# A fused attention and feed-forward kernel: two more slots between the mask and the exponential from the seventh pair on

## The chip, the cores and the metric

The kernel runs on one NeuronCore of a Trainium2 chip. The metric is the device time of one execution in microseconds (us). Engine names are those of the profile: PE (TensorE, matrix products; PEld are its weight loads), ACT (ScalarE), DVE (VectorE), POOL (GpSimd), and SP, which here only issues DMAs. Each engine works through its own instructions in program order; semaphores order them against each other.

## The reference, cut to what matters

Attention with a threshold over 8 batches of 8 heads, 576 positions and 64 channels; its output goes through a feed-forward layer of 512 to 2048 to 512.

```
scores = scale * q @ k.T                          # 8 x 8 x 576 x 576
thresh = max(scores, -1) - tau
scores = where(scores >= thresh, scores, -1e9)
attn   = exp(scores - max(scores, -1)); attn /= sum(attn) + 1e-9
x      = heads side by side (attn @ v)            # 4608 x 512
h      = x @ w_in;  g = h - tanh(h);  out = g @ w_out
```

## The kernel before

**Tiles.** Heads are taken in pairs, 4 pairs to a batch, 32 pairs in all. A pair has 9 score tiles of 128 query rows by 576 keys (`TPP = 9`): eight regular ones and one in which both heads share the rows (64 each). So there are 288 tiles, numbered through. Two neighbouring tiles, an even one (kind A) and an odd one (kind B), make a *duo*: they share one mask result `z`, one turned tile `zT`, one `pT`.

**Steps of a tile.** `scores` (L387): PE forms the scores in high and low halves in PSUM (`psS`, from `kT` and the swapped copy `kS`), and DVE scales them into `sc` and takes the row maximum in the same instruction (L420). `shift` (L426): DVE makes the bias `nb`. `kink` (L439): ACT applies the threshold with a very steep Prelu and writes `z` (L447). Then `z` has to be turned so that keys lie on partitions. For the first six pairs (`on_pe`, L57) PE does that in `weights` (L466), and ACT's exponential reads PSUM (L475). From the seventh pair on (tiles 54 and up) `kink` of the odd tile issues one DMA transpose for the duo on the SP queue into a buffer of `zt_pool` (L454), and `weights` is one exponential for the duo on ACT (L483). `attend` (L488): PE multiplies by v into `psO` (L506, L513, L524). `norm` (L531) divides on DVE, `emit_x` (L551) turns the result on PE for the layer.

**The layer.** It works in blocks of 512 tokens, one per batch, and a last block of leftovers. An *h* step is four products into `psH` (L579), then tanh on ACT (`bend`, L592) and the subtraction on DVE (`shrink`, L598) into `g`. A *y* step is four products into `psY` (L605); every fourth is followed by a copy on DVE (L617) and a store issued on SP (L620). `PATTERN` writes by hand in which slot of a 36-slot block (four pairs) an h or a y stands; '-' is a slot with neither.

**The order of work** is one loop over slots (L852). Slot s does, in this order: scores of tile s + `AHEAD`; `kink` of tile s + `MASK`; `weights` of tile s + `SOONER` of its pair; the layer's step; the stores; `attend` of the tile whose weights were two slots (`LAG`) before; then whatever `plan` holds. A shared tile of kind A is put off one slot, so every 18 slots one slot has no scores and the next has two tiles of them. `plan` holds the preparation of q, k and v (loads, splitting on POOL in L228 to L232, turning, swapping `kT` into `kS` on POOL in L337), placed relative to `AHEAD`; so are the weights' loads. From the tenth pair on q and k are turned by DMA transposes on SP too (L315).

Counted from the slot of a tile's own scores, the steps before the change are:

| pairs | mask | exponential | attend |
|---|---|---|---|
| 1 to 4 | +3 | +4 | +6 |
| 5 and 6 | +3 | +8 | +10 |
| 7 to 32 | +3 | +8 | +10 |

The first layer block starts at slot 40 (when tile 48 is scored), each next block 36 slots later; after the last slot the remaining layer steps follow without attention.

Of the kernel before, what the change touches and what calls it, by code (L numbers as in the profile page):

```python
# [18 lines left out]
def kernel(  # L19
# [26 lines left out]
    HPAIR = H // 2  # L46
# [6 lines left out]
    NTILE = NPAIR * TPP  # L53
# [6 lines left out]

    W = 2 * S

    AHEAD = 8
    LDK = 16
    MASK = 5
    LAG = 2


# [30 lines left out]
    for i in range(6):  # L99
# [8 lines left out]
    pool = lambda name, bufs, **kw: ctx.enter_context(  # L108
        tc.tile_pool(name=name, bufs=bufs, **kw)
    )  # L110
# [3 lines left out]
    qk_pool = pool("qk", 3)  # L114
    sc_pool = pool("sc", AHEAD - MASK + 2)
    st_pool = pool("st", 12)
    z_pool = pool("z", 4)
    zt_pool = pool("zt", 6)
    p_pool = pool("p", 3)
    o_pool = pool("o", 2)  # L120
    wt_pool = pool("wt", 4)
# [218 lines left out]
    def turn_first(t, part):  # L340

        hl = hls[0, t[0]]
        c0, c1 = ((0, 5), (5, TPP))[part]
        pl, tag = (ps_y, "y") if t == "ks" else (ps_h, "h")
        ps = pl.tile([P, 5 * P], FP16, name=f"ps1_{t}", tag=tag)
        for c in range(c0, c1):
            o = ps[:, (c - c0) * P : (c - c0 + 1) * P]
            if t == "ks":
                for a in range(2):
                    turn_chunk(o[64 * a : 64 * a + 64, :], c, hl[:, c, 1 - a, :])  # L350
            else:
                turn_chunk(o, c, hl[:, c, :, :].rearrange("p a d -> p (a d)"))
        if part == 0:
            mats[0, t] = qk_tile(t)
        dst, n = mats[0, t][:, c0 * P : c1 * P], (c1 - c0) * P
        if part == 1 or t == "q":
            nc.scalar.copy(out=dst, in_=ps[:, 0:n])
        else:
            nc.vector.tensor_copy(out=dst, in_=ps[:, 0:n])
# [17 lines left out]
    def kind(i):  # L377

        return "AB"[i % 2]

    def place(i):

        p, j = divmod(i, TPP)
        j = j - p % 2
        return (p, None, 4) if j in (-1, 8) else (p, j // 4, j % 4)

    def scores(i):  # L387
        p, hh, t = place(i)
        qT, kT, kS = mats[p, "q"], mats[p, "k"], mats[p, "ks"]
        ps = ps_big.tile([P, 1024], F32, name="psS", tag="big")  # L390
        main, rem, lo = slice(0, 512), slice(512, 576), 0
        if kind(i) == "B":
            main, rem, lo = slice(512, 1024), slice(448, 512), 448
        if hh is None:
            qrem = REM
            if q_by_dma(p):
                qrem = (slice(512, 640, 2), slice(513, 640, 2))
            for n, kk in enumerate((kT, kS)):
                for dst, cols in ((main, main_keys), (rem, rem_keys)):
                    for hh in range(2):  # L400
                        nc.tensor.matmul(  # L401
                            out=ps[64 * hh : 64 * hh + 64, dst],
                            lhsT=qT[:, qrem[hh]], rhs=cols(p, kk, hh),
                            start=(n == 0), stop=(n == 1),
                        )
        else:
            lhs = qT[:, (5 * hh + t) * P : (5 * hh + t + 1) * P]
            for n, kk in enumerate((kT, kS)):
                for dst, cols in ((main, main_keys), (rem, rem_keys)):
                    nc.tensor.matmul(  # L410
                        out=ps[:, dst], lhsT=lhs, rhs=cols(p, kk, hh),
                        start=(n == 0), stop=(n == 1),
                    )
        sc = sc_pool.tile([P, S], F32, name="sc")
        if kind(i) == "B":
            mx = mxs[i] = mxs.pop(i - 1)
        else:
            mx = mxs[i] = mx3[i // 2 % len(mx3)]
        c = int(kind(i) == "B")
        nc.vector.tensor_scalar(  # L420
            out=sc, in0=ps[:, lo : lo + S], scalar1=SC, scalar2=None,
            op0=ALU.mult, op1=ALU.max, accum_out=mx[:, c : c + 1],
        )
        scs[i] = sc

    def shift(i):  # L426

        if kind(i) == "A":
            return
        mx = mxs.pop(i)  # L430
        nb = st_pool.tile([P, 9], F32, name="nb", tag="nb")
        nc.vector.tensor_scalar(  # L432
            out=nb.rearrange("p (a b) -> p a b", b=3)[:, :, 0:2],
            in0=mx.rearrange("p (a b) -> p a b", b=4)[:, :, 0:3],
            scalar1=-1.0, scalar2=tau, op0=ALU.mult, op1=ALU.add,
        )
        nbs[i - 1], nbs[i] = nb[:, 0:1], nb[:, 1:2]

    def kink(i):  # L439
        sc, nb = scs.pop(i), nbs.pop(i)  # L440
        if kind(i) == "B":
            zt = zs.pop(i - 1)
            z = zt[:, S:W]
        else:
            zt = zs[i] = z_pool.tile([P, W], BF16, name="z")
            z = zt[:, 0:S]
        nc.scalar.activation(  # L447
            out=z, in_=sc, func=ACT.Prelu, bias=nb, scale=1.0, alpha=STEEP
        )
        if on_pe(i):  # L450
            zts[i] = zt
        elif kind(i) == "B":
            zts[i] = zt_pool.tile([P, TPP, P], BF16, name="zT")
            nc.sync.dma_start_transpose(out=zts[i], in_=zt)  # L454
# [148 lines left out]
    def project(m, ms, part, ps, last, cols=slice(0, d_model)):  # L603
# [30 lines left out]
    LAST = 1  # L634

    PATTERN = lambda m: {
        0: '-h--h-hh--h-hh-h-hh-h--hh-h--hh-y-yy',
        B - 2: 'hyhyhyhyhyhyhyhyhyhyhyhyhyhyhyhy',
    }.get(m, 'h-yhyhhyhyyhyyhh-yhhyhhy-yhyyh-yyhhy')

# [88 lines left out]
    def w_cast():  # L729
        flat, wt, i, cols = loaded.pop(0)  # L730
        nc.gpsimd.tensor_copy(out=flat[:, i * cols : (i + 1) * cols], in_=wt)
# [52 lines left out]
    for p in range(DUAL, NPAIR):  # L784
        first = TPP * p - AHEAD
        at = lambda d, f: plan.setdefault(first - d, []).append(f)
# [11 lines left out]
    for p in range(1, DUAL):  # L798
        first = TPP * p - AHEAD
        for d, f in PREP[3 if p == 1 else 0 :]:  # L800
# [37 lines left out]
    for at in sorted(plan):  # L838
        if at < -AHEAD:
            plan.setdefault(-AHEAD, []).extend(plan.pop(at))  # L840

    SOONER = (4, 4, 4, 4, 0, 0, 0)
    kinks, wts, atts = {}, {}, {}
    for i in range(NTILE + 3):
        at = i - SOONER[min(i // TPP, 6)]
        atts.setdefault(at + LAG, []).append(i)
        if i < NTILE:
            wts.setdefault(at, []).append(i)  # L850
            kinks.setdefault(i // 2 * 2 + 2 - AHEAD if i < 4 else i - MASK, []).append(i)
    for s in range(-AHEAD, NTILE + LAG + 3):  # L852
        p, j = divmod(max(s, 0), TPP)
        if 0 <= s < NTILE and j == 2 + LAG and p % HPAIR == 0 and p >= HPAIR:
            assert not todo
            todo = [(s + i, step) for i, step in layers(stage, False, PATTERN(stage))]
            stage += 1
        if s == NTILE:
            todo = [(s + n, step) for n, step in enumerate(layers(stage, True))]
            stage += 1  # L860
        if 0 <= s + AHEAD - 1 < NTILE:
            shift(s + AHEAD - 1)

        n = s + AHEAD
        if 0 < n < NTILE and place(n)[1] is None and kind(n) == "B":
            scores(n - 1)
        if 0 <= n < NTILE and (place(n)[1] is not None or kind(n) == "B"):
            scores(n)
        if s == 1 - AHEAD:
            for t in ("k", "q", "ks"):  # L870
                turn_first(t, 1)
        for i in kinks.pop(s, []):
            kink(i)
        bend()
        for i in wts.pop(s, []):
            weights(i)
        while todo and todo[0][0] <= s < NTILE + FIRST:
            todo.pop(0)[1]()
        if s == 0:
            nc.vector.tensor_tensor(  # L880
                out=fold, in0=ident_bf[:, 0:64], in1=ident_bf[:, 64:P], op=ALU.add
            )
        shrink()
        for store in going:
            store()
        going = stores[:-1]
        del stores[:-1]
        for i in atts.pop(s, []):
            pp, jj = divmod(i, TPP)
            if i < NTILE:  # L890
                attend(i)
                odd = pp % 2
                if jj == 3 + odd:
                    norm(pp, 0)
                elif odd and jj in (0, 8):
                    norm(pp - (jj == 0), 1)
            if pp and jj == 1 + pp % 2:
                emit_x(pp - 1)
        for step in plan.pop(s, []):
            step()  # L900
        for _ in range(cast_when.count(s + AHEAD)):
            w_cast()
        for _ in range(load_when.count(s + AHEAD)):
            w_load(next(pieces))
# [56 lines left out]
```

## Time and profile before

| | us |
|---|---|
| three runs | 511.88, 507.43, 510.61 |
| median | 510.61 |
| the profiled execution | 504.09 |
| its span, first to last instruction | 502.3 |

| engine | busy us | share of the span | instructions |
|---|---|---|---|
| PE | 482.5 | 96% | 4292 |
| PEld | 270.5 | 54% | 4354 |
| ACT | 431.9 | 86% | 617 |
| DVE | 400.8 | 80% | 1151 |
| POOL | 292.2 | 58% | 390 |

The profile is of one execution. Matmuls overlap, so the mean length of one (379 ns for 512 columns) is longer than the distance from one to the next. The costliest groups of the page are the row maximum on DVE (L420, 288 times, mean 752 ns), the mask on ACT (L447, 288 times, 773 ns), the y products (L605, 373 ns), the duo's exponential (L483, 117 times, 1157 ns), the h products (L579, 379 ns) and the score products (L410).

### The profile page before, as it was taken

Reading aid. Unit: us, or ns where it says so; the run is one execution under the profiler, and the core shown is the slowest. Engines: PE = TensorE matmul, PEld = TensorE weight load, DVE = VectorE, ACT = ScalarE, POOL = GpSimd, SP = SyncE. Lnnn points to the kernel's source line nnn. Section 1 sums busy time; section 2 is a strip of 40 time slices with the busy share of each in tenths; the row PEclk is TensorE's granted clock in tenths of the full one; section 3 lists DMA queues with packets and bytes.
Section 4 is the critical chain, followed back from the end, with each engine's and each line's share of the span. In section 5 each row is a group of like instructions: output and inputs, shape, how many; then the busy total and the mean of one; then the engine's idle time right before and its main releaser. Section 6 shows DMA issues by size and latency. Waiting matters only on the chain.

```text
span 502.3 us, 12201 instructions
## 1 busy us (share of the span) xinstructions
PE 482.5 (96%) x4292; PEld 270.5 (54%) x4354; DVE 400.8 (80%) x1151; ACT 431.9 (86%) x617; POOL 292.2 (58%) x390
## 2 busy tenths in 40 slices
PE   8999899989999999999999999999999999999997
PEld 4667566555555555555555555555555555444444
DVE  5899978988889898988898889889888887544430
ACT  5999999899999999999999999999989999434330
POOL 8999999897765675576575765658556600000000
PEclk9999999999999999999999999999999999999999
DMA  6852558999999999999999999999999965311003
GB/s 208 261 162 91 189 167 229 209 202 229 223 207 243 247 246 222 223 251 212 239 218 249 247 213 215 258 217 249 235 196 228 226 119 116 88 42 43 36 29 84
DMA packets 232157, 95.02 MB, mean 189 GB/s; under 512 B 202784, under 2 KB 221472, under 8 KB 232096
## 3 DMA queue, kind: packets, MB, share of 16 engines
q1 hardware_dynamic: 211152, 72.58, 75.4%
q10 hardware_dynamic: 20944, 21.67, 15.7%
q8 instruction: 34, 0.56, 0.5%
q14 instruction: 27, 0.22, 0.1%
HBM read 36.70 MB, written 9.44 MB: 92 GB/s over the span
## 4 chain that ended last, share of the span: by engine, by line
PE 74%; POOL 9%; ACT 5%; issue 4%; DVE 4%; DMA 2%; SPq 1%; ACTq 0%; POOLq 0%
PE psY L605 23%; PE psH L579 19%; PE psS L410 18%; PE psO L513 5%; PE psHt L579 3%; DMA kraw<-in_k_dram 2%; PE psS L401 2%; POOL kS L337 2%; ACT z L447 2%; DVE sc L420 1%; PE psO L524 1%; ACT pT L483 1%; ACT pT L475 1%; DVE g L598 1%; PE psO L506 1%
## 5 line engine op out<-in xcount | busy, mean ns | idle before, releaser
L420 DVE TENSOR_SCALAR_CACHE_REDUCE sc<-psS 128x576 f32<-128x576 f32 x288 | 213.5, 752 | 25.5 <-PE psS L410 12.4
L447 ACT ACTIVATE z<-sc,nb 128x576 bf16<-128x576 f32 x288 | 217.3, 773 | 8.6 <-DVE nb L432 6.1
L605 PE MATMUL psY<-w_out_sb,g 128*128 128x512 bf16 (+1 forms) x564 | 140.8, 373 | 1.6 <-issue 0.2
L483 ACT ACTIVATE pT<-zT 128x1152 f16<-128x1152 bf16 x117 | 135.4, 1157 | 4.8 <-DMA zT<-z 3.3
L579 PE MATMUL psH<-xT,w_in_sb 128*128 128x512 bf16 x448 | 118.8, 379 | 4.2 <-issue 1.7
L337 POOL COPY kS<-kT 64x1152 f16<-64x1152 f16 x62 | 70.9, 1144 | 76.6 <-DMA kT<-khl 72.8
L598 DVE SCALAR_TENSOR_TENSOR g<-th,psH 128x512 bf16<-128x512 f32 x128 | 87.6, 684 | 27.3 <-ACT th L592 26.3
L410 PE MATMUL psS<-kT,qT 128*128 128x512 f16 (+1 forms) x512 | 104.4, 285 | 3.2 <-DVE sc L420 1.9
L410 PE MATMUL psS<-kS,qT 128*128 128x512 f16 (+1 forms) x512 | 104.6, 286 | 0.0
L410 PEld LDWEIGHTS <-qT 128*128 128x128 f16 x1024 | 72.5, 97 | 57.8 <-issue 4.1
L592 ACT ACTIVATE th<-psH 128x512 f32<-128x512 f32 x128 | 74.9, 585 | 20.9 <-PE psH L579 20.9
L605 PEld LDWEIGHTS <-g 128*128 128x128 bf16 x592 | 51.1, 98 | 54.6 <-DVE g L598 0.4
L579 PEld LDWEIGHTS <-w_in_sb 128*128 128x128 bf16 x576 | 49.0, 98 | 55.9 <-issue 4.6
L513 PE MATMUL psO<-vb,pT 128*128 128x65 bf16 x1024 | 53.3, 194 | 0.0
L513 PEld LDWEIGHTS <-pT 128*128 128x128 f16 x1024 | 44.2, 98 | 10.0
L232 POOL TENSOR_TENSOR qhl<-qraw,qhl 128x576 f16<-128x576 f32 x31 | 39.7, 1282 | 2.6
L232 POOL TENSOR_TENSOR khl<-kraw,khl 128x576 f16<-128x576 f32 x31 | 39.7, 1281 | 2.6
L475 ACT ACTIVATE pT<-psZ 128x512 f16<-128x512 bf16 (+1 forms) x54 | 35.1, 653 | 2.5 <-PE psZ L466 2.2
L617 DVE COPY yo<-psY 128x512 f32<-128x512 f32 (+1 forms) x31 | 21.1, 679 | 13.0 <-PE psY L605 12.4
L539 DVE TENSOR_TENSOR osb<-psO,rc 128x256 bf16<-128x256 f32 x64 | 27.2, 425 | 2.2
L506 PE MATMUL psO<-vb,pT 128*128 128x130 bf16 x128 | 28.1, 220 | 0.1
L228 POOL TENSOR_SCALAR qraw<-qraw 128x576 f32<-128x576 f32 x31 | 20.9, 673 | 12.5 <-DMA qraw<-in_q_dram 12.5
(77 smaller groups left out, 453.0 us busy)
## 6 DMA issues: line engine op xcount, KB each, us to landing
out_dram<-yo SPq DMA_DIRECT2D x32, 256.0 KB, 3.6
kraw<-in_k_dram ACTq DMA_DIRECT2D x24, 288.0 KB, 4.5
qraw<-in_q_dram ACTq DMA_DIRECT2D x24, 256.0 KB, 4.3
wt<-in_moe_w_in_dram SPq DMA_DIRECT2D x8, 512.0 KB, 4.3
wt<-in_moe_w_out_dram SPq DMA_DIRECT2D x8, 512.0 KB, 4.3
vraw<-in_v_dram ACTq DMA_DIRECT2D x24, 160.0 KB, 4.1
vraw<-in_v_dram ACTq DMA_DIRECT2D x24, 128.0 KB, 3.9
vraw<-in_v_dram SPq DMA_DIRECT2D x8, 256.0 KB, 3.5
```

The costliest lines, as they stand in the source:

```text
L232: nc.gpsimd.tensor_tensor(out=hl[:, :, 1, :], in0=x, in1=hl[:, :, 0, :], op=ALU.subtract)
L337: nc.gpsimd.tensor_copy(out=o, in_=i)
L410: nc.tensor.matmul(out=ps[:, dst], lhsT=lhs, rhs=cols(p, kk, hh), start=(n == 0), stop=(n == 1),)
L420: nc.vector.tensor_scalar(out=sc, in0=ps[:, lo : lo + S], scalar1=SC, scalar2=None, op0=ALU.mult, op1=ALU.max, accum_out=mx[:, c : c + 1],)
L447: nc.scalar.activation(out=z, in_=sc, func=ACT.Prelu, bias=nb, scale=1.0, alpha=STEEP)
L475: nc.scalar.activation(out=pt[:, off * P : (off + n) * P], in_=ps[:, 0 : n * P], func=ACT.Exp)
L483: nc.scalar.activation(out=pt[:, 0 : n * P], in_=zts.pop(i)[:, 0:n, :], func=ACT.Exp)
L513: nc.tensor.matmul(out=po[:, t - 1 + ab, :], lhsT=pt[:, blk * P : (blk + 1) * P], rhs=vb[:, hh, c, :], start=False, stop=(n == 7), skip_gr ...
L579: nc.tensor.matmul(out=ps, lhsT=w_in_sb[:, c, n * P : (n + 1) * P], rhs=xs[m][:, c, :] if m < B else xR[:, c, :, :], start=(c == 0), stop= ...
L592: nc.scalar.activation(out=th, in_=ps, func=ACT.Tanh)
L598: nc.vector.scalar_tensor_tensor(out=gs[m][:, n, :], in0=th, scalar=-1.0, in1=ps, op0=ALU.mult, op1=ALU.add,)
L605: nc.tensor.matmul(out=ps, lhsT=gs[m][:, n, ms * P : (ms + 1) * P], rhs=w_out_sb[:, n, cols], start=(n == 0), stop=(n == DF_C - 1),)
```

## The change

Scores go ten slots ahead instead of eight, and the mask seven instead of five. `SOONER` grows by two for the first six pairs, so that these keep their distances: in the table above their rows stay as they are. From the seventh pair on `SOONER` is 0 as before, so there the exponential comes 10 slots after the scores and the attend step 12. `zt_pool` has eight buffers instead of six; `sc_pool` keeps its five (`AHEAD - MASK + 2`). The first layer block starts at slot 38, which is again when tile 48 is scored, and its pattern is two slots longer, with its last three y steps later by one, two and two slots; the other blocks still start at slots 76, 112 and so on, now two slots later against the scores. The loop has two slots more. No instruction is added or removed; POOL's instructions keep their order.

```
-    AHEAD = 8
+    AHEAD = 10
-    MASK = 5
+    MASK = 7
...
-    zt_pool = pool("zt", 6)
+    zt_pool = pool("zt", 8)
...
     PATTERN = lambda m: {
-        0: '-h--h-hh--h-hh-h-hh-h--hh-h--hh-y-yy',
+        0: '-h--h-hh--h-hh-h-hh-h--hh-h--hh--y--yy',
...
-    SOONER = (4, 4, 4, 4, 0, 0, 0)
+    SOONER = (6, 6, 6, 6, 2, 2, 0)
...
-        if 0 <= s < NTILE and j == 2 + LAG and p % HPAIR == 0 and p >= HPAIR:
+        if 0 <= s < NTILE and j == LAG + 2 * (p > HPAIR) and p % HPAIR == 0 and p >= HPAIR:
```

## The prediction

> **What bounds the kernel now.** I read the slices of the page first, then the busy time by stretches, then the chain of waits, and last who waits for the duos' DMA. A slot is one score tile.
>
> ```profile
> 20.00:40.00 20.00, 18.47 (x264) 13.27 (x262) 17.91 (x57) 19.69 (x34) 18.76 (x24) 1.00 0.58 180
> ...
> 100.00:120.00 20.00, 18.04 (x169) 10.12 (x172) 17.10 (x54) 19.89 (x27) 17.02 (x21) 1.00 1.04 213
> 120.00:150.00 30.00, 29.63 (x260) 16.19 (x264) 26.15 (x79) 29.50 (x42) 21.13 (x29) 1.00 1.20 216
> 150.00:380.00 230.00, 227.08 (x2017) 124.91 (x2051) 203.27 (x600) 222.68 (x304) 149.55 (x190) 1.00 1.22 233
> 380.00:430.00 50.00, 48.77 (x415) 26.69 (x421) 40.16 (x116) 46.79 (x64) 13.50 (x18) 1.00 0.87 172
> 430.00:490.00 60.00, 59.68 (x292) 27.41 (x296) 27.42 (x44) 23.11 (x38) 0.00 (x0) 1.00 0.10 36
> ```
>
> Columns: stretch, its length, busy us of PE, PEld, DVE, ACT, POOL, granted clock, DMA share, GB/s. Until 120 us no engine is full: PE has 1.5 to 2 us idle in 20, while ACT is at 98 to 99%. From 120 us on PE is busy 98.7 to 99.5%, ACT 97%. The clock is 1.00 throughout. A busy PE may still be a slow one, so I checked it by the chain of waits:
>
> ```profile
> 108.37 1.15 POOL kS L337
> 109.52 0.04 issue
> 109.56 1.16 POOL kS L337
> ...
> 110.86 1.16 ACT pT L483
> ...
> 115.95 0.65 PE psS L410 x4
> ...
> 141.03 1.11 PE psS L401 x16
> ...
> 144.40 0.86 PE psY L605 x4
> ...
> 154.88 0.98 PE psS L410 x8
> ...
> 193.91 1.11 PE psS L401 x16
> ...
> 246.79 1.11 PE psS L401 x16
> ```
>
> Columns: start, us on the chain, what. Up to 110.7 us the chain runs through POOL (preparation of the ninth and tenth pairs), then ACT and DVE, and from 115.95 us on through PE alone. It repeats every 193.91 − 141.03 = 52.88 us, then 246.79 − 193.91 = 52.88: one block of 36 slots, so a slot is 1.47 us. What PE must do in a block, by the chain's own rows: 32 regular score tiles at 0.98/2 = 0.49 (15.7), 4 shared at 1.11/2 (2.2), 32 layer steps at 0.86 (27.5), 16 attend duos at 0.06 + 0.26 (5.1), 20 shared attend products at 0.059 between starts (1.2), 4 turns at 0.25 (1.0): 52.7 us. Of 52.88 us PE has 0.2 us free. That is the first thing to know of this change: between 116 and 430 us nothing that shortens a wait elsewhere can give more than about 6 blocks x 0.2 = 1.2 us.
>
> The wait that the change is nearest to:
>
> ```profile
> PE psH L579 <- issue: 1.6, 10, 0.2
> ...
> ACT pT L483 <- DMA zT<-z: 3.3, 7, 0.8
> ```
> ```profile
> DMA to landing us min/median/max: 3.2/4.7/7.4
> ```
>
> Total us, times, longest, from 120 to 400 us. Seven of 117 exponentials wait for their turned duo, 3.3 us together. In the same stretch PE waits for no engine: its only row is issue.
>
> **The change part by part.** Sums go against the profiled execution, 504.09 us (span 502.3 and 1.8 around it). It lies 6.5 us under the median of the three runs, 510.61; I carry the difference that I find over to the median.
>
> *More room between mask and exponential.* Now 5 slots x 1.47 = 7.35 us lie between them, of which the mask takes 0.77 and SP's queue and the DMA the rest; afterwards 10.3 us. The longest landing seen, 7.4 us, then fits. So the 3.3 us of ACT's waits should go. They end on ACT, which has 3% free, while PE shows no wait for `pT`; worth 0 to 1.2 us (all that PE has free), I take 0.3.
>
> *Two more zT buffers.* A buffer is held for 7 slots instead of 5, that is 4 duos instead of 3; six buffers would have done and eight do. Cost 0; were they short, SP would hold back the transposes of q and k behind them.
>
> *The first six pairs, mask, preparation, POOL, weights.* All move together with `AHEAD`. Against the scores nothing changes; cost 0 until tile 54 is masked.
>
> *The seam.* From tile 54 on attend and from the second block on the layer lag the scores by two slots more. This happens at about 88 us (first duo exponential at 89.5) to 120 us (tile 84 is scored at 120.0, which is where the second block began). PE's work is not lost, it is put off: one attend duo (0.32) and 2 slots of layer at 32/36 x 0.86 (1.53), together 1.85 us. If PE ran full there, putting off would be free, since the scores of two slots would come in earlier and be saved at the end. But it is not full: 18.04 of 20 us. POOL paces the stretch up to 110.7 us and its work per tile is unchanged, so tile 84 comes no sooner, and PE idles for what was taken away: +1.85 us. If instead ACT paces it (19.89 of 20), ACT is relieved of one exponential, 1.16 us, and the rest is +0.7. If PE fills the gap, 0. The chain shows POOL for most of the stretch and ACT and DVE for its last 5 us; I take +1.2, bounds 0 and +1.85.
>
> *SP's queue.* The store of a block's row group moved from between two duo transposes to just ahead of the transpose of the next pair's k. It holds SP for some 0.55 us (230.41 to 230.99 us in the time line), and kT lands as much later, qT behind it. `kS` is ready 2.9 to 8.3 us before the pair's first score tile, qT 0.5 to 5.2 us. At one pair (the 30th, 0.5 us) it could show: 0 to +0.2, I take 0.
>
> *The alignment within a block.* The slot without scores and the slot with two shared tiles meet the hand-written pattern at steps 12/13 and 30/31 instead of 14/15 and 32/33. Before, DVE's two row maxima fell into the slot of a `norm` (0.43 + 0.34 + 0.19 us); now they don't. With PE at 52.7 of 52.88, a gain is at most part of the 1.2 us above; a loss is the second rival. I take 0.
>
> *The end.* Scores end two slots earlier, the last ten slots hold attend and layer alone. From 380 to 430 us PE has 1.2 us idle, waiting for `g` and for the last `xT`; these distances are unchanged. −0.6 to +0.6, I take 0. The steps after the last slot are the same.
>
> Sum: 1.2 − 0.3 = **+0.9 us**: 505.0 for an execution like the profiled one, 511.5 for the median.
>
> A rule to weigh. The profile's row is 292 products in the 60 us after 430 us, 0.86 us for four, and 52.7 of 52.88 us in a block: PE is full. The Trainium skill, Perfetto Trace Analysis, "Identifying the Most-Contended Engine", says that matmul occupancy does not tell how far a kernel is from its limit and to use LDWEIGHTS' busy share; here that is 54%, so by the rule PE would have room and the exponential's earlier start could shorten the kernel by the 3.3 us of waits, 507.3. I go by the distances between products.
>
> **The rivals.**
>
> *A, no change (0.64):* the sum above; 511.5. With bounds −0.6 and +2.5 for the sum and the runs' own spread (−3.2 to +1.3 about the median) it gives 507.5 to 514.
>
> *B, the turned duos land later in ordinary executions than in the profiled one (0.21):* that could be what the 6.5 us between 504.09 and 510.61 are. For it: besides the seven that waited, eight more of the 117 exponentials started within 0.2 us of their landing, and ACT has only 3% to spare: if each DMA took 1 us longer, 35 of 117 would wait, 0.6 us on average, 21 us of waits against 0.03 x 310 = 9 us of free ACT time. After the change a landing 2.9 us later would still be covered. Against it: nothing in the profile shows a later landing, and a spread of three runs can come from anything. It would give back up to 6.5 us: 504.1 + 0.9 = 505.0, with half of it 508.
>
> *C, slower (0.15): the slot without scores now falls on '-'* (step 30). PE then has at most an attend (0.32 us) before the two shared tiles, and the second needs the `psS` of the tile scored just before, which DVE must have read (0.75 + 0.08 us). If DVE lags by more than the 0.86 us of that tile's own layer step plus the attend and the first shared tile (0.55), PE stands. It decides when DVE is over 0.9 us late at step 29. Each time costs up to 0.83 us; twice a block over some six blocks makes 6 to 10 us with the seam: 517 to 520; if it occurs only at step 30, 6 x 0.83 + 1.2 = 6.2, 516.8. Against it: from 120 to 400 us PE never waits for DVE's row maximum, and DVE waits for PE's scores 14.5 us.
>
> The change does what it says: the distances follow from the slots. What could undo it is SP being late with the issue itself; that is within A.
>
> **How the numbers follow.** About 1%, 5.1 us, is what a measurement of this kernel can tell from no change. Faster by more needs 505.5 or less: half of B (0.12) and the low edge of A's spread (0.06), 0.18. Slower by more needs 515.7: most of C (0.12) and A's high edge (0.03), 0.15. The rest, 0.67. The range takes A and most of B and leaves out C and B's lower edge: 505 to 515.
>
> **What would show it.** Right: the row of ACT's exponential waiting for zT gone or under 0.5 us; the block still repeats every 52.9 us by the shared score tiles in PE's chain; PE idle between 85 and 122 us up by 0.5 to 2 us; the start of PE's unbroken chain one to three us later; span 502 to 505. B is shown by runs near 505 with the profile's span unchanged; C by a row of PE waiting for DVE's row maximum and a period over 53.5 us. I would be wrong if the period falls below 52.5, which would mean that PE's cost per step is not what I took, or if the seam costs over 3 us.

## The result and the profile after

| | before | changed |
|---|---|---|
| median of 15 runs, us | 509.01 | 513.84 |
| spread, us | 504.93 to 511.88 | 510.25 to 516.35 |
| the profiled execution, us | 504.09 | 511.58 |
| its span, us | 502.3 | 509.4 |

The ratio is 1.0117, 95% interval 1.0089 to 1.0146. A second comparison of the same two kernels (below) gave 1.0081, 1.0028 to 1.0133. So the change makes the kernel about 1% slower. The forecast was 511.5 us, range 505 to 515. Every ratio here is to executions of the kernel before that were timed beside the run, and it leaves out executions in a slower state, which the medians include.

Busy time by stretches after the change (columns as before):

```profile
100.00:120.00 20.00, 17.78 (x162) 9.54 (x163) 17.64 (x57) 19.89 (x27) 16.29 (x20) 1.00 1.05 205
120.00:150.00 30.00, 29.74 (x266) 16.38 (x270) 25.84 (x78) 29.61 (x41) 19.78 (x26) 1.00 1.24 219
150.00:380.00 230.00, 223.68 (x1966) 123.10 (x2003) 199.88 (x585) 219.01 (x299) 146.50 (x187) 1.00 1.20 229
380.00:430.00 50.00, 48.64 (x421) 26.30 (x426) 41.51 (x121) 46.79 (x64) 18.51 (x24) 1.00 0.96 173
```

The stretch that was full is not full any more: from 150 to 380 us PE is busy 223.68 us instead of 227.08. The chain of waits shows it by the block's period (start, us, what):

```profile
140.47 1.11 PE psS L401 x16
194.28 1.11 PE psS L401 x16
...
247.74 1.11 PE psS L401 x16
301.95 1.11 PE psS L401 x16
357.10 1.11 PE psS L401 x16
```

The blocks take 53.81, 53.46, 54.21 and 55.15 us, where each took 52.88 to 52.90. What PE waits for from 116 to 430 us (us, times, longest):

```profile
PE psS L401 <- DMA qT<-qhl: 2.3, 3, 1.2
PE psS L410 <- DMA qT<-qhl: 1.3, 4, 0.5
PE psH L579 <- DVE g L598: 1.0, 2, 0.6
```

Waits for the turned q are new. They go with the times of the transposes of q (first line before, second after), in the answer for the tile qT:

```profile
DMA to landing us min/median/max: 3.3/3.8/6.0
```
```profile
DMA to landing us min/median/max: 3.5/5.8/8.0
```

The exponential's own wait, the one that the change aimed its two slots at, is gone; its group on the page ends with 0.0 us of idle time:

```profile
L483 ACT ACTIVATE pT<-zT 128x1152 f16<-128x1152 bf16 x117 | 134.8, 1152 | 0.0
```

Part of it has moved to the instruction in front. Four buffers hold `z` (`z_pool`, unchanged), so the mask of the fourth duo after a given one needs the buffer that the DMA transpose of the first may still be reading. With seven slots between mask and exponential, that mask stands in the slot of the late duo's exponential, ahead of it on ACT, and now it waits instead:

```profile
ACT z L447 <- DMA zT<-z: 2.3, 4, 1.0
```

The kernel before had no such row. The mask's group on the page (first line before, second after):

```profile
L447 ACT ACTIVATE z<-sc,nb 128x576 bf16<-128x576 f32 x288 | 217.3, 773 | 8.6 <-DVE nb L432 6.1
```
```profile
L447 ACT ACTIVATE z<-sc,nb 128x576 bf16<-128x576 f32 x288 | 216.9, 770 | 15.4 <-DVE nb L432 4.9
```

ACT's idle time ahead of mask and exponential together was 13.4 us (8.6 and 4.8) before and is 15.4 us after.

**A measure that adds up.** Matmul records can be missing and matmuls overlap, but all profiles here hold the same 4354 weight loads, one for each product. With the time from one start to the next that each kind shows in the full stretch (216 ns for 512 columns, 109 for 256, 56 for 128, 57 to 58.5 for 130, 32 for 65, 28 for 64, half of it for the score products of the shared tiles, which run two at a time), the loads stand for 472.9 us of PE work in every kernel. What is left of a stretch is called PE's idle time here; time that PE loses by running slower is in it too. The small overlaps make it good to some tenths of a us. The last copy and store, some 4 us without products, are in the third column.

| PE idle, us | to 120 us | 120 to 420 us | after | span |
|---|---|---|---|---|
| before | 20.7 | 4.1 | 4.6 | 502.3 |
| before, second profile (e8) | 20.7 | 11.3 | 4.9 | 509.8 |
| changed | 22.4 | 9.1 | 5.0 | 509.4 |
| changed, second profile (e9) | 21.7 | 7.4 | 4.4 | 506.4 |
| e1, pattern turned back | 21.9 | 7.7 | 4.4 | 506.9 |
| e3, q loads later | 21.7 | 6.6 | 4.2 | 505.4 |
| e2, only the layer later | 22.1 | 17.4 | 6.0 | 518.4 |

Two things stand out: delaying the layer costs 1.0 to 1.7 us before 120 us, and executions of one kernel differ by as much as the change does. Spans are therefore used below to see where time goes, and timed ratios to say how much.

### The profile page after: what moved, and what is told of

Its sections match the earlier page's. It is cut to its first block, busy times and chain, and to the rows that moved or that the text cites. A ratio compares the mean times of both kernels' runs of the same rounds, so it can differ in the third digit from the quotient of the medians.

```text
span 509.4 us, 12158 instructions
## 1 busy us (share of the span) xinstructions
PE 486.1 (95%) x4287; PEld 271.8 (53%) x4354; DVE 402.2 (79%) x1151; ACT 433.5 (85%) x617; POOL 291.4 (57%) x390
## 4 chain that ended last, share of the span: by engine, by line
PE 60%; DMA 12%; DVE 2%; ACT 2%; issue 1%; SPq 1%; ACTq 0%; DVEq 0%
PE psY L605 21%; PE psH L579 15%; PE psS L410 14%; DMA qT<-qhl 9%; PE psO L513 3%; PE psHt L579 3%; PE psS L401 2%; DMA zT<-z 2%; DMA out_dram<-yo 1%; PE psO L524 1%; ACT z L447 1%; PE psO L506 1%; DVE sc L420 1%; DVE g L598 1%; PE psX L556 1%
## 5 line engine op out<-in xcount | busy, mean ns | idle before, releaser
L447 ACT ACTIVATE z<-sc,nb 128x576 bf16<-128x576 f32 x288 | 216.9, 770 | 15.4 <-DVE nb L432 4.9
```

The source lines that it names most:

```text
L447: nc.scalar.activation(out=z, in_=sc, func=ACT.Prelu, bias=nb, scale=1.0, alpha=STEEP)
```

## The experiments

Three theories were to be told apart: that the layer steps now meet the preparation (loads and transposes of q and k) at other places (alignment); that the longer distance itself costs; that only the seam at 85 to 120 us does.

**e1: pattern turned back by two.** The changed kernel with

```
-    }.get(m, 'h-yhyhhyhyyhyyhh-yhhyhhy-yhyyh-yyhhy')
+    }.get(m, 'yhyhhyhyyhyyhh-yhhyhhy-yhyyh-yyhhyh-')
```

> The changed kernel, with the hand-written pattern of blocks 2 to 6 turned by two steps, so that each h and y meets the same score slot, q load and q transpose as before the change; mask, exponential and attend keep their new distances. If the alignment of layer steps with the preparation is what makes the turned q late: the block repeats every 52.9 to 53.3 us again, PE waits under 1.5 us for qT, the profile's span is 503 to 506 us. If the longer distance itself (more duos under way, attend later) costs the time: period 53.5 to 55, span 508 or more. If only the seam costs: period as in the changed kernel.

Measured: 508.70 us, ratio to before 0.9982, 0.9944 to 1.0019. The slowdown is gone with the longer distance still there. The waits of PE from 116 to 430 us:

```profile
PE psX L556 <- DVE g L598: 2.7, 5, 0.9
PE psH L579 <- DVE g L598: 1.0, 3, 0.4
```

None is for qT, whose landing is at a median of 4.2 us (5.8 with the change, 3.8 before). The period was 53.49 us, above what I expected: the turned pattern puts an h step into the slot in which the attention output is turned, and psX then waits for a buffer that g has to free, about 0.6 us a block. So alignment is what costs, and the distance does not. The times show this, not the period: in the second profile of the changed kernel (e9) most blocks are no longer than here. What the turned pattern restores shows on SP: the duos' transposes were issued 0.2 us after the end of their mask before (median of 117), 1.5 us after it with the change, and 0.2 us here.

**e2: only the layer later.** The kernel before with

```
-        0: '-h--h-hh--h-hh-h-hh-h--hh-h--hh-y-yy',
+        0: '-h--h-hh--h-hh-h-hh-h--hh-h--hh--y--yy',
...
-        if 0 <= s < NTILE and j == 2 + LAG and p % HPAIR == 0 and p >= HPAIR:
+        if 0 <= s < NTILE and j == 2 + LAG + 2 * (p > HPAIR) and p % HPAIR == 0 and p >= HPAIR:
...
-            todo = [(s + n, step) for n, step in enumerate(layers(stage, True))]
+            todo += [(s + 2 + n, step) for n, step in enumerate(layers(stage, True))]
```

> The kernel before, with only the layer blocks from the second on begun two slots later (the first block's pattern as in the change); scores, mask, exponential, attend and zT buffers as before. Alignment theory: qT of every second pair lands 6 to 8 us after its issue, the block period is 53.5 to 55 us, 4 to 7 us slower than before. Distance theory: period 52.9, only the seam's 1 to 2 us slower.

Measured: 522.87 us, 1.0276 (1.0189 to 1.0364): slower even than the change. The delay of the layer alone does harm, but not as I expected: the transposes of q land in 4.2 us, and PE waits little for them. Its exponentials wait for the turned duos (total us from 116 to 430 us, times, longest), though only 0.5 us of PE's own waits name the exponential; the largest, 3.9 us, is for DVE's row maximum:

```profile
ACT pT L483 <- DMA zT<-z: 12.8, 13, 2.1
```

At this alignment the longer distance seems to be worth something: the changed kernel has the same delay of the layer, waits for turned duos of 2.3 us in place of 12.8, and is 1.6% faster than e2 (1.0276 to 1.0117). The attend steps also stand two slots apart in the two, so this is not the distance's worth alone.

**e3: q loads of every second pair one slot later.** The changed kernel with, for odd pairs from the eleventh counted from zero on,

```
-            ("kt", 10), ("qt", 6), ("k0", 18), ("q0", 14), ("v0", 15),
-            ("q1", 13), ("v1", 12), ("ks", 11), ("qs", 8), ("vs", 6),
+            ("kt", 10), ("qt", 6), ("k0", 18), ("q0", 13), ("v0", 15),
+            ("q1", 12), ("v1", 12), ("ks", 11), ("qs", 8), ("vs", 6),
```

> The changed kernel, with the two q loads of every second pair (issued on ACT's queue) one slot later, so that they start about 1.5 us later behind the transpose of the other pair's q. If those loads are what the transpose shares the DMA engines with: its latency at even pairs falls from 6 to 8 us to under 5.5, PE's waits for qT go, period under 53.3, 3 to 6 us faster than the changed kernel. If the transpose is late because SP issues it late, or the distance itself costs: within 1.5 us of the changed kernel.

Measured: 510.15 us, 1.0012 (0.9968 to 1.0056): the slowdown is gone, by moving two loads. How they meet the transpose of q is seen on the issue queues. Pair 26 in the changed kernel (start, us, queue and instruction):

```profile
335.90 1.55 SPq L315 DMA_TRANSPOSE qT<-qhl  x1
336.29 0.41 ACTq L175 DMA_DIRECT2D qraw<-in_q_dram  x1
336.78 0.64 ACTq L175 DMA_DIRECT2D qraw<-in_q_dram  x1
```

That transpose landed at 343.43, 7.5 us after its issue, and the scores waited for it at 343.5. The same pair before:

```profile
332.68 1.61 SPq L315 DMA_TRANSPOSE qT<-qhl  x1
333.93 1.18 ACTq L175 DMA_DIRECT2D qraw<-in_q_dram  x2
```

There it landed after 3.6 us. Over the ten even pairs from 12 to 30 (medians): the two loads followed the transpose after 1.5 and 2.6 us before, after 0.4 and 0.8 us with the change, and after 0.2 and 2.9 us in e3; the transposes took 4.3, 7.4 and 5.9 us, and q was ready before the pair's first scores by 3.5, 0.1 and 0.9 us. So in e3 one of the two loads still meets the transpose, the other no longer does. What PE still waits for q there:

```profile
PE psS L401 <- DMA qT<-qhl: 0.7, 1, 0.7
```

The latency stayed over the 5.5 us that I had expected, and it is no shorter than in the second profile of the changed kernel (5.7 us in e9, with q ready about 1.3 us early). So the times show that the place of the loads matters; that it acts through the landing of q alone is not shown. On SP nothing was restored: the duos' transposes were issued 1.5 us after their mask, as with the change, so that delay alone is not what costs.

The Trainium skill, DMA: Bandwidth & Descriptors, "Issuing engines are not separate DMA queues", says that DMAs of different issuing engines run on the same 16 engines and mix there. The traces agree as far as they go: where the loads on ACT's queue followed more closely, the transposes on SP's took 7.4 us (5.7 in the second profile) instead of 4.3. That sharing the engines is the reason is not shown here.

**e4: the mask one slot earlier in the kernel before.**

```
-    MASK = 5
+    MASK = 6
```

> The kernel before, with the mask one slot earlier (two slots after the scores instead of three), so that mask and exponential lie 6 slots apart and nothing of the layer or attend moves. If late landings of the turned duos cost time in ordinary executions (the prediction's rival B): 2 us or more faster than before. If the slack is worth nothing because PE is full: within 2 us of before, with ACT's 3.3 us of waits for zT mostly gone.

Measured: 534.69 us, 1.0486 (1.0419 to 1.0553). A miss: the mask then comes too close to the scores, and ACT, working in order, stands before it:

```profile
ACT z L447 <- DVE nb L432: 37.7, 74, 1.9
```

That was 6.1 us before. The room has to be made on the other side of the mask, as the change does, so this run says nothing on its worth.

**e5 and e7: the kernel before with those q loads one slot earlier, and one slot later.** e5 changes `q0` from 14 to 15 and `q1` from 13 to 14, e7 to 13 and 12, in the lines shown for e3.

> The kernel before, with the two q loads of every second pair one slot earlier, and nothing else: it makes in the old kernel the meeting that the change made, q loads issued within 1 us behind the other pair's q transpose. Collision theory: the transpose's median latency at even pairs rises from 4.3 to 6 us or more, its slack falls under 1.5 us, 2 to 6 us slower than before. If the loads don't matter: within 1.5 us of before.

> The kernel before, with the two q loads of every second pair one slot later. If the collision already costs something in ordinary executions of the old kernel: 1 to 3 us faster than before. If PE is full there and q has slack enough: within 1.5 us, with POOL's wait for the raw q up.

Measured: e5 513.65 us, 1.0129 (1.0029 to 1.0230); e7 512.67 us, 1.0065 (1.0022 to 1.0107). In e5 the two loads did not come to stand where the change put them: the first was issued 1.6 us ahead of the transpose, the second 1.8 us behind it (medians). The transposes of q took 5.7 us (median of the ten pairs), but q was still ready 2.5 us early, and PE did not wait for it; it waited 3.0 us for exponentials whose turned duos were late. The kernel before shows such waits without any edit (e8 below), so they do not explain the loss. The times say that the place of these loads matters in the old kernel too; the way is open. e7 shows that the old place was good for the old kernel: later is worse as well.

**e6: stores at another place.** The changed kernel, each store 7 slots after its copy, so that on SP it stands between two duo transposes:

```
-        for store in going:
-            store()
-        going = stores[:-1]
-        del stores[:-1]
+        held += [(s + 7, store) for store in stores]
+        stores.clear()
+        while held and held[0][0] <= s:
+            held.pop(0)[1]()
```

> The changed kernel, with each output store issued 7 slots after its copy instead of after the next copy, so that it stands between two duo transposes on SP's queue again and not just ahead of the transpose of k. If the store's place is what delays q: qT latency at even pairs under 5.5 us, 3 to 6 us faster than the changed kernel. Collision theory of the q loads: within 1.5 us of the changed kernel, latency stays 6 to 8 us.

Measured: 515.02 us, 1.0130 (1.0063 to 1.0196): as the changed kernel. The store ahead of the transpose of k is not the cause. The transposes of q took 6.4 us here (median of the ten pairs), yet PE waited for them only 0.4 us, and 3.5 us for DVE's row maximum:

```profile
PE psS L410 <- DVE sc L420: 3.5, 8, 1.1
```

So the slow alignment can cost as much with hardly a wait for q.

**e8 and e9: both kernels once more, for a second profile.**

> The kernel before once more, to see where an ordinary execution differs from the profiled one of 504.1 us. If it is the front (first loads): the block period is 52.9 us again. If it is late transposes: periods over 53 us and waits of PE for qT or of ACT for zT over 3 us. If it is PE's clock: a granted clock under 1.00.

> The changed kernel once more, since one profiled execution of the kernel before was no ordinary one. Collision theory: again the transposes of q at even pairs take 6 to 8 us, PE waits for qT, and no exponential waits for zT; periods 53.4 to 55.5 us; PE idle about 4 us between 100 and 120 us. If the late q belonged to that one execution: latency near 4.5 us and the time lost elsewhere. Time about 1.2% over before.

e8 took 511.58 us, e9 508.59 us in the profiled execution and 513.12 in the median, 1.0081 (1.0028 to 1.0133). e8 shows what the first profile of the old kernel hid. Its front is the same to a tenth (20.7 us idle to 120 us). What differs is the landing of the turned duos (first line on ACT, over the whole span; second on PE, 116 to 430 us):

```profile
ACT pT L483 <- DMA zT<-z: 11.1, 12, 2.7
```
```profile
PE psO L506 <- ACT pT L483: 2.2, 1, 2.2
```

3.3 us had become 11.1, and one of these waits reached PE. The granted clock was 0.997 over the span, and the time at a lower clock lies in one place, just behind that wait (first line before, second e8; the clock is the column after POOL's):

```profile
384.00:388.00 4.00, 3.82 (x33) 2.00 (x32) 3.50 (x12) 4.00 (x6) 2.54 (x3) 1.00 1.58 247
```
```profile
384.00:388.00 4.00, 3.67 (x22) 1.46 (x22) 3.06 (x8) 4.00 (x6) 2.58 (x4) 0.57 1.13 249
```

By my estimate from these rows that costs PE another 1.7 us (0.43 of 4 us), so e8 is not an execution with late duos alone. e9 repeats the changed kernel's signs, weaker: the loads follow the transposes of q after 0.2 and 0.7 us, these take 5.7 us (median of the ten pairs), and PE waits for them:

```profile
PE psS L401 <- DMA qT<-qhl: 1.3, 1, 1.3
PE psS L410 <- DMA qT<-qhl: 0.7, 1, 0.7
```

No exponential waits for zT in it, but two masks do:

```profile
ACT z L447 <- DMA zT<-z: 2.8, 2, 1.8
```

ACT's idle time ahead of mask and exponential together is 14.0 us in e9, and 20.4 us in e8. The blocks of e9 took 53.12, 52.99, 52.98 and 54.57 us.

**f1, f2, f3: a version to beat both.** f1 is e1 with h steps moved off the slots in which the attention output is turned; f2 has the loads of e3 as well; f3 is f1 with `pool("zt", 6)`.

```
+    }.get(m, 'yhyhhyhyyyhyhh-yhyhhyh-yhyhy-yyhhyh-')
```

> The changed kernel with the pattern turned by two as in e1_pattern_back, and h steps moved off the three slots in which the attention output is turned (there psX waited for a buffer that g had to free, 0.6 us a block). If the longer distance is a gain that the alignment had hidden: the period is 52.9 us, no exponential waits for zT, 3 to 5 us faster than before, 7 to 10 faster than the changed kernel. If the distance is worth nothing and only the seam is left: 1 to 3 us slower than before.

> The kernel of f1_new_pattern with the two q loads of every second pair one slot later as well. With the alignment restored, q has 3 us of slack at even pairs: within 1.5 us of f1_new_pattern. If the loads still collide there: 2 us or more faster than it.

> The kernel of f1_new_pattern with six buffers for turned duos instead of eight. Four duos are held at a time, so six should do: within 1 us of f1_new_pattern. If six are too few: SP's transposes wait for exponentials, 2 us or more slower.

Measured: f1 513.93 us, 1.0109 (1.0072 to 1.0145); f2 519.11, 1.0163 (1.0106 to 1.0219); f3 518.71, 1.0159 (1.0093 to 1.0224). A failure. The psX wait is gone as meant, but three y steps in a row made another:

```profile
PE psY L605 <- DVE yo L617: 4.8, 5, 1.5
```

There is one buffer for `psY`, and the next row group cannot begin before DVE has copied the last one out. So f1 does not test the worth of the distance. f2, with the loads moved as in e3, is no faster than f1, so the move helps at one alignment and not at any. f3's interval overlaps f1's, so the runs leave open whether six buffers differ from eight. In the profile of the changed kernel each duo's transpose was issued 6.0 us or more after the end of the exponential that freed the sixth buffer back, so six would have been free in time.

## Why the prediction was right and wrong

**The size.** The time lies in the range and on the side of the forecast, but +0.9 us became +4.8 (+3.6 in the second comparison): 0.95% by the medians, 1.17% by the ratio, 0.81% in the second. That is at the 1% line beyond which I had given a chance of 0.15. That it still fell into the range is partly luck, since the cause of most of it was no part of the sum. Two signs that I had named for being right failed: the blocks did not keep to 52.9 us, and the spans were 509.4 and 506.4 us, not 502 to 505. Rival A's range was also added up too narrowly: its own terms give 506.8 to 514.4, not 507.5 to 514.

**The seam: right.** Forecast +1.2 us, bounds 0 and +1.85. PE's idle time up to 120 us rose from 20.7 to 21.7, 21.7, 21.9 and 22.4 us in e9, e3, e1 and the changed kernel; 0.5 us of the last one's was there already at 60 us.

**SP's store: right in its cost, wrong as the place to look.** I took 0 for it, and e6 agrees with that within its interval. I had written the room of q beside it, 0.5 to 5.2 us, and used it only against the store's 0.55 us.

**The step that failed: "All move together with AHEAD. Against the scores nothing changes; cost 0".** In slots that is true. But a load issued on ACT's queue starts when ACT gets to it, and a transpose on SP's when what stands before it there has been issued; both hang on which layer steps stand in the slots around them. The pattern moved by two slots against the preparation, and a gap of 1.5 us between transpose and load became 0.4. My part on alignment looked at PE and DVE alone and not at the two issue queues. e1 (pattern back) and e3 (two loads moved) each remove the whole slowdown within their intervals, and e3 does so with the layer steps where the change put them against the scores. That the h steps in ACT's queue set the gap is read from the code and not shown by itself: medians against the pair's first scores say that the transpose was issued 1.0 us later and the load 0.2 us earlier. I had named SP being late with the issue, and given it no cost; it was late by 1.5 us instead of 0.2.

**More room between mask and exponential: the exponential's row went to zero as forecast, but the wait went partly to the mask, and its worth was taken from the wrong execution.** I counted the buffers of `zT` and not the four of `z`. I also set the longest landing, 7.4 us, against the new distance of 10.3 us; from the end of the mask to the landing, SP's queue included, it took up to 10.9 us with the change (12.1 in e9, 7.5 before). I took the profiled execution, with 3.3 us of waits and a full PE, for an ordinary one. It was a quick one: 504.09 us, where only two of the 15 runs above were under 507. Rival B had the mechanism right (e8: 11.1 us of waits, blocks of 52.9 to 55.4 us), but not the balance: I let it be paid out in full, without the loss at the same queues. Some 1.7 us of what sets e8 apart is its lower clock. How much the distance gains in ordinary executions is not pinned down: e1 stands at 0.9982 with the seam's 1 us and 2.7 us of psX waits in it, and e2 suggests more.

**Rival C: did not happen.** PE waited 0.2 us for DVE's row maximum from 116 to 430 us. The step without scores on '-' costs nothing that shows.

**What stays open.** The waits for qT that the profiles name, 3.6 and 2.0 us, and the seam's 1 us make up most of a difference of 3.6 to 4.8 us, less what the shorter waits gave back. But e6 is as slow with 0.4 us of them, so the wait that carries the loss is not settled. The sum cannot be closed, since profiled executions of one kernel lie up to 7.5 us apart. Part of the difference may be the clock: in nine of the changed kernel's 15 runs above the mean granted clock was 0.995 to 0.998 (median 514.22 us), in the other six 0.999 or more (512.28 us). For the kernel before, these 15 have no clock on record; in the second comparison it was 0.998 or less in 4 of 13 runs before and 4 of 10 after.

## What to carry to other kernels

When a schedule is shifted against itself, list every DMA whose issue stands in a compute engine's queue and see what it now follows: moving two loads by a slot, or the pattern by two steps, was worth as much as the whole change here. A wait that disappears is a gain only if no other transfer has become the late one, and if it did not move to the instruction in front, which may need another buffer of the same transfer. And one profile gives the place of a wait, not its usual size: where the runs spread by 1%, look at a second profile before taking a quiet one for the rule.

## What the runs showed of the hardware

The landing of DMA transposes varies from execution to execution of one program: the kernel before had 3.3 us of waits for them in one profile and 11.1 in another, with landings of the turned duos of 4.7 us in the median and 7.4 at most in the one, 5.1 and 9.4 in the other, and with the front identical to a tenth of a us.

Among all the profiles here PE had a gap of over 2 us between 120 us and the end of its work in two, 2.2 us each: e8 at 381 us and e4 at 348 us. Each was followed, 0.9 and 1.4 us after its end, by 3.4 us at a granted clock of 0.5. No other profile shows a lower clock there, though they have gaps of 1.0 to 1.8 us. So in these traces a stop of PE of 2.2 us came with a second loss of about 1.7 us (an estimate: half of 3.4).
